# Re-layout reads of queries and keys: two of three row groups by one transfer

## The chip, the cores and the metric

The kernel runs on one core of one Trainium2 chip. The core has a matrix engine (TensorE, PE in the profile; its weight loads are PEld), a vector engine (DVE), a scalar engine (ACT), GpSimd (POOL) and SyncE (SP), which here only issues transfers; ACT issues some, too. All transfers run on 16 DMA engines. Each engine works through its own instructions in order and waits at semaphores for the others. The metric is device time in microseconds of one execution; the median of several runs is compared.

## The reference

One transformer layer on a prompt of 2048 tokens with 640 features, in float32:

```python
qkv = (layernorm(x) @ wqkv).reshape(B, S, 3, H, Dh)     # S=2048, H=32, Dh=20
scores = einsum("bhqd,bhkd->bhqk", q, k) * Dh ** -0.5
mask: 0 <= query - key < 256
h = x + (softmax(masked scores) @ v) @ wo
out = h + (gelu(layernorm(h) @ w_gate) * (layernorm(h) @ w_up)) @ w_down   # F=1536
```

Attention looks back over at most 256 keys, so a block of 128 queries needs its own block of keys and the two before it.

## The kernel before, in words

**Tiles.** Tokens are handled in 16 blocks of 128 (`B[j]`) and, for the projections of queries and keys, in 8 chunks of two blocks (`C[c]`, 256 columns, `CW`). Float32 operands are split in a high and a low float16 part, and a product is made of three: high by high, high by low, low by high.

**From projection to attention.** `qk(c, which)` computes the queries (`which` 0) or keys (1) of a chunk, 640 feature rows by 256 token columns, in three pieces. `qk_out` turns each into its two float16 parts and writes them, by transfers issued on ACT, to a DRAM tensor `d` of shape [640, 2, 256]: feature row, high or low, token. The weight columns are permuted so that the row is (a, d, i), with a the parity of the head (2), d the feature inside the head (20) and i the pair of heads (16).

`stack(c, which, d)`, the function of this change, reads `d` back in another layout. The tiles `qT` (one per chunk, two in turn) and `kT` (a ring of six blocks) have 128 rows. Rows 0 to 59 belong to the even heads, rows 64 to 123 to the odd ones: three groups of 20 rows, one row for each feature of a head. Along a row lie 16 heads of 256 tokens each. The groups of `qT` hold high, high, low and those of `kT` high, low, high, so one product over 60 rows gives all three terms. Rows 60 and 61 of `qT` later receive the rows' maxima in two parts (`max_transpose`, a small transfer on ACT), against a constant in `kT`. Each of the three groups of each half is one transfer: six for `qT`, six for `kT`, twelve per chunk. One transfer has 20 rows of 16 runs of 256 float16, 512 bytes each.

**Use.** `maxima` multiplies a block's queries with its window of keys to find the row maxima (DVE), `scores` makes the scores in transposed form for ACT's exponential, `value_lane` multiplies with the values, and `wo_block` projects and adds the residual. Afterwards the feed-forward runs over chunks of 512 tokens; it needs neither `qT` nor `kT`.

**What sets the order.** The whole order of instructions is made before the run. Lanes (generators) offer their next step with the engines that it needs and a function of when its data will be ready; the main loop at the end of `block_kernel` picks one step at a time. The class `Clock` keeps the planner's estimate of each engine's time: a transfer costs bytes / 150,000 us on a common line for 2-byte data on the chip, its issue 0.35 or 0.75 us, and no more than eight are thought of as in flight. In `stack` a first wait holds until the data is in DRAM and older blocks are scored (`B[2 * c - 3].scored`), so that the ring of `kT` has room; from chunk 2 on each transfer also waits until the line has at most `PACE` = 1 us of work left. When both stacks of a chunk are issued, its blocks go to the queue of `maxima`. All instructions pass through one helper, `call` in class `Engine`, so the profile gives line 199 for nearly all of them, and tiles tell them apart.

**On SP's queue**, in one order, stand these reads, the loads of x and of the weights, the turns of x to feature rows (transposing transfers), the loads of the residual and the writes of h. ACT issues the writes to `d` and the maxima.

Of the kernel before, what the change touches and what calls it, by code (L numbers as in the profile page):

```python
# [21 lines left out]
S, D, H, DH, F = 2048, 640, 32, 20, 1536  # L22
# [5 lines left out]
CW = 2 * P  # L28
# [225 lines left out]
def block_kernel(ctx: ExitStack, tc: tile.TileContext, x, wqkv, wo, wg, wu, wd, out):  # L254
    nc = Clock(tc.nc)
# [54 lines left out]
    def need(*reads, slots=(), when=None, eng="tensor"):  # L310

        def f():
            if when and not when() or any(opened[n] >= banks[n] for n in slots):
                return INF
            return max([nc.ready(reads, eng)]
                       + [nc.slot(psums[n], n, banks[n]) for n in slots])
        return f
# [432 lines left out]
    def qk_out(c, which, ts, ps, d, left):  # L750

        o = ps[:, :len(ts) * CW].rearrange("p (t n) -> p t n", n=CW)
        up = qs if c == which == 0 else _pow2(QE)
        yield on("scalar", ps, when=lambda: pos["qk"] < pos["qks"] + 2 and (c or pos["qs"]))
        pos["qk"] += 1
        st = nc.tile(wq, [P, 2, 2, CW], F16, "qks", 2)
        hi, lo = (st[:, :len(ts), i, :] for i in range(2))
        nc.scalar.activation(hi, o, AF.Copy, scale=up)
        yield on("vector", hi, after=ps)
        nc.vector.scalar_tensor_tensor(lo, o, up, hi, op0=ALU.mult, op1=ALU.subtract)  # L760
        done("mm")
        both = st[:, :len(ts)].rearrange("p t m n -> p t (m n)")
        yield on("scalar", both)
        nc.scalar.dma_start(d[ts[0] * P:(ts[-1] + 1) * P].rearrange("(t p) m n -> p t (m n)", p=P),
                            both)
        pos["qks"] += 1
        left[0] -= 1
        if not left[0]:
            side.append((LATE, stack(c, which, d)))

    def stack(c, which, d):
        yield ("sync",), need(d, when=lambda: pos["big"] == 2 and (W["q"].ready if c < 2 else
                                                                B[2 * c - 3].scored), eng="sync")
        if which == 0:
            C[c].qT = at("qT", [P, H // 2, CW], F16)
            for b in (2 * c, 2 * c + 1):
                B[b].mx = at("mxs", [P, H], F32, 4)
            to = C[c].qT
        else:
            s = 2 * c % RK  # L780
            to = kT[:, :, s:s + 2, :].rearrange("p i r n -> p i (r n)")
        for par in range(2):
            for m, i in enumerate(((0, 0, 1), (0, 1, 0))[which]):
                rows = slice(64 * par + DH * m, 64 * par + DH * m + DH)
                if c > 1:
                    yield ("sync",), lambda: nc.moved["sync"] - PACE
                nc.sync.dma_start(to[rows], d.rearrange("(a d i) m n -> a m d i n", a=2,
                                                        d=DH)[par, i])
        C[c].stacked += 1
        if C[c].stacked == 2:  # L790
            for b in (2 * c, 2 * c + 1):
                for pr in range(0, H // 2, pairs(b)):
                    heapq.heappush(maxq, (b, pr))
# [29 lines left out]
    def pairs(j):  # L823

        return 2 if j < 2 else 1
# [82 lines left out]
    def row_lane():  # L908
        while True:
            yield ("tensor",), row_need  # L910
            for f, n in list(row):
                f(n)
# [714 lines left out]
    rows = Lane(row_lane())  # L1627
# [89 lines left out]
```

## Time and profile before

| | |
|---|---|
| median of 3 runs | 1019.06 us (1015.35 to 1019.22) |
| the profiled execution | 1015.33 us, span 1013.6 us |
| mean granted TensorE clock | 0.997 |
| PE busy | 996.3 us, 98% of the span |
| DVE, ACT, POOL busy | 754.7, 442.5, 315.0 us |
| attention, by the use of qT and kT | to 566 us of the span |
| re-layout reads | 48 to qT, 48 to kT, 160 KB each |

How to read it: the page gives busy time per engine, then the chain of work that ended last, then the costliest groups. A row of a timeline is start, duration, engine (with a q: the engine's sequencer, as where it issues a transfer), line, operation, output<-inputs, shape and count; in brackets the idle time before it and what ended it. A row of a chain is start, duration and what. A row of a window table is the stretch and its length, busy time and instruction count of PE, PEld, DVE, ACT and POOL, then the granted clock, the DMA engines' mean share and GB/s. A row of the transfer view is queue, packets, MB and the packets' time as a share of 16 engines; the digits above it are tenths of that share in 40 slices.

### The profile page before, as it was taken

The page shows a single profiled execution, that of the slowest core. Times are in us where ns is not written, and L with a number is a line of the kernel's source. Part 1 is how long each engine was busy: PE and PEld are TensorE (multiplying, and loading weights), DVE is VectorE, ACT ScalarE, POOL GpSimd, SP SyncE. Part 2 cuts the span into 40 slices and gives each one's busy share as a digit, 9 for nine tenths or more (in the row PEclk, how much of TensorE's full clock was granted, in tenths as well). Part 3 has the DMA queues.
Part 4 walks back from the last instruction along what each step waited for, and adds up shares of the span by engine and source line. Part 5 has one row for each costly group of instructions (what it writes and reads, how often), then busy time and mean ns, then how long its engine had stood idle before and what let it go on. Part 6 is the DMA issues. An engine that isn't in the chain of part 4 may idle for free.

```text
span 1013.6 us, 30516 instructions
## 1 busy us (share of the span) xinstructions
PE 996.3 (98%) x12798; PEld 696.4 (69%) x12798; DVE 754.7 (74%) x2212; ACT 442.5 (44%) x711; POOL 315.0 (31%) x504
## 2 busy tenths in 40 slices
PE   8999999999999999999999999999999999999998
PEld 7876777666666776776655654577777777777776
DVE  7888999786667877676688687798888875544553
ACT  5516666654555555554567634432222212221220
POOL 7004344643344333332345311254313300000000
PEclk9999999999999999999999999999999999999999
DMA  8658775291271714236004342323453542222211
GB/s 308 148 127 177 185 163 167 67 166 41 71 133 39 143 55 88 64 79 188 18 29 133 68 130 92 98 107 116 144 187 102 148 142 78 79 103 80 78 53 52
DMA packets 105834, 112.67 MB, mean 111 GB/s; under 512 B 38368, under 2 KB 79584, under 8 KB 105696
## 3 DMA queue, kind: packets, MB, share of 16 engines
q1 hardware_dynamic: 93600, 99.97, 36.7%
q10 hardware_dynamic: 12096, 10.75, 3.5%
q8 instruction: 100, 1.64, 0.7%
q14 instruction: 38, 0.31, 0.1%
HBM read 73.73 MB, written 28.84 MB: 101 GB/s over the span
## 4 chain that ended last, share of the span: by engine, by line
PE 86%; DVE 7%; DMA 3%; ACT 2%; issue 1%; SPq 1%; POOL 0%; ACTq 0%; DVEq 0%
PE mm L199 44%; PE pv L199 12%; PE ra L199 12%; PE rb L199 10%; PE tp L199 7%; DVE junk L199 1%; DMA kT<-qk 1%; SPq L199 1%; DVE am L199 1%; DMA wst<-in_wu_dram 1%; DMA qT<-in_wqkv_dram 1%; DMA wst<-in_wg_dram 1%; ACT pt L199 1%; DVE ht L199 0%; DVE w1l L199 0%
## 5 line engine op out<-in xcount | busy, mean ns | idle before, releaser
L199 POOL TENSOR_SCALAR_AFFINE_SELECT pt<-pt 128x512 f32<-128x512 f32 x352 | 174.8, 512 | 297.0 <-ACT pt L199 281.3
L199 DVE CUSTOM_DVE_ANT_0 junk<-rb,band 128x320 bf16<-128x320 f32 x228 | 111.5, 489 | 53.4 <-PE rb L199 48.8
L199 ACT ACTIVATE pt<-ra,esc 128x640 f32<-128x640 f32 (+2 forms) x132 | 100.6, 770 | 74.3 <-PE ra L199 69.3
L199 DVE CUSTOM_DVE_ANT_0 junk<-ra,band 128x320 bf16<-128x320 f32 x220 | 107.7, 489 | 33.2 <-PE ra L199 26.8
L199 ACT ACTIVATE pt<-rb,esc 128x640 f32<-128x640 f32 (+2 forms) x124 | 94.1, 764 | 82.4 <-PE rb L199 73.2
L199 PE MATMUL pv<-pt,v 128*21 128x128 f32 x2880 | 104.7, 279 | 0.0
L199 PEld LDWEIGHTS <-ah 128*128 128x128 f16 x768 | 75.1, 98 | 29.2 <-issue 1.9
L199 ACT ACTIVATE gel<-gel,ffk 128x512 f32<-128x512 f32 x36 | 26.0, 722 | 134.3 <-DVE gel L199 134.3
L199 PEld LDWEIGHTS pv<-pt,v 128*21 128x21 f32 x2880 | 70.0, 101 | 9.9 <-issue 1.0
L199 PEld LDWEIGHTS <-ws 128*128 128x128 f16 x720 | 70.5, 98 | 8.1
L199 PEld LDWEIGHTS <-qT 60*64 60x64 f16 x1280 | 29.8, 104 | 61.0 <-issue 51.9
L199 PEld LDWEIGHTS <-kT 62*64 62x64 f16 x2880 | 63.4, 107 | 11.2 <-issue 7.5
L199 PEld LDWEIGHTS <-gu 128*128 128x128 f16 x440 | 41.9, 98 | 36.1 <-issue 2.5
L199 DVE SCALAR_TENSOR_TENSOR ht<-mm,ffk,ht 128x320 f32<-128x320 f32 x96 | 52.1, 545 | 13.7 <-PE mm L199 11.8
L199 ACT CAST ah<-gel 128x512 f16<-128x512 f32 x48 | 29.6, 617 | 68.7 <-DVE gel L199 68.6
L199 PE MATMUL mm<-xh,w1h 128*128 128x256 f16 x200 | 54.6, 273 | 0.8 <-DVE qks L199 0.8
L199 PE MATMUL mm<-xl,w1h 128*128 128x256 f16 x200 | 54.7, 274 | 0.0
L199 PE MATMUL mm<-xh,w1l 128*128 128x256 f16 x200 | 54.6, 273 | 0.0
L199 POOL TENSOR_TENSOR gelt<-gelt 128x256 f32<-128x256 f32 x18 | 15.3, 852 | 112.0 <-ACT gelt L199 111.9
L199 PE MATMUL mm<-w3h,oh 128*128 128x320 f16 x160 | 48.3, 302 | 1.4 <-DVE qks L199 1.4
L199 PE MATMUL mm<-w3l,oh 128*128 128x320 f16 x160 | 48.2, 301 | 0.0
L199 PE MATMUL mm<-w3h,ol 128*128 128x320 f16 x160 | 48.1, 300 | 0.0
(313 smaller groups left out, 2562.6 us busy)
## 6 DMA issues: line engine op xcount, KB each, us to landing
ws<-wsums SPq DMA_DIRECT2D x24, 640.0 KB
qk<-qks ACTq DMA_DIRECT2D x32, 256.0 KB
qT<-qk SPq DMA_DIRECT2D x48, 160.0 KB
kT<-qk SPq DMA_DIRECT2D x48, 160.0 KB
wsums<-ws SPq DMA_DIRECT2D x12, 640.0 KB
ht<-in_x_dram SPq DMA_DIRECT2D x16, 320.0 KB
h_dram<-ht SPq DMA_DIRECT2D x16, 320.0 KB
ht<-h_dram SPq DMA_DIRECT2D x16, 320.0 KB
```

Source lines behind the costliest of these rows:

```text
L199: r = real(*args, **kw)
```

## The change

For each half, the first two row groups are read by one transfer of 40 rows, the third by one of 20 as before. For `kT` the source is high and then low, read with the part as the outermost dimension; for `qT` it is the high part twice, a broadcast with an outermost dimension of step 0 and size 2. A chunk has 8 reads in place of 12: four of 320 KB, four of 160 KB. The bytes that land, and where, are the same.

```diff
+        parts_ = d.rearrange("(a d i) m n -> a m d i n", a=2, d=DH)
         for par in range(2):
-            for m, i in enumerate(((0, 0, 1), (0, 1, 0))[which]):
-                rows = slice(64 * par + DH * m, 64 * par + DH * m + DH)
+            for m, n in ((0, 2), (2, 1)):
+                rows = slice(64 * par + DH * m, 64 * par + DH * (m + n))
+                if n == 2:
+                    src = parts_[par] if which else parts_[par, 0].unsqueeze(0).to_broadcast(
+                        [2, DH, H // 2, CW])
+                else:
+                    src = parts_[par, 1 - which]
                 if c > 1:
                     yield ("sync",), lambda: nc.moved["sync"] - PACE
-                nc.sync.dma_start(to[rows], d.rearrange("(a d i) m n -> a m d i n", a=2,
-                                                        d=DH)[par, i])
+                nc.sync.dma_start(to[rows], src)
```

## The prediction, made before the change was run

> **What bounds the kernel now.** I read the page first, for the shares, the chain that ended last and the transfers.
>
> ```profile
> span 1013.6 us, 30516 instructions
> PE 996.3 (98%) x12798; PEld 696.4 (69%) x12798; DVE 754.7 (74%) x2212; ACT 442.5 (44%) x711; POOL 315.0 (31%) x504
> ...
> PE 86%; DVE 7%; DMA 3%; ACT 2%; issue 1%; SPq 1%; POOL 0%; ACTq 0%; DVEq 0%
> ...
> qk<-qks ACTq DMA_DIRECT2D x32, 256.0 KB
> qT<-qk SPq DMA_DIRECT2D x48, 160.0 KB
> kT<-qk SPq DMA_DIRECT2D x48, 160.0 KB
> ```
>
> TensorE works in 98% of the span, in an order that the planner wrote before the run. It has 1013.6 - 996.3 = 17.3 us of idle time, so a product that waits for late data is paid nearly in full: nothing behind it on TensorE can pass it. What matters is how much room each of the 96 re-layout reads (48 of qT, 48 of kT, 160 KB each) has before TensorE needs it. So I read SP's timeline for the issue of the reads, all eight qT stacks and the last reads of chunk 3's kT:
>
> ```profile
> 29.43 5.47 SPq L199 DMA_DIRECT2D qT<-qk  x6
> 61.82 6.16 SPq L199 DMA_DIRECT2D qT<-qk  x6
> 119.78 6.73 SPq L199 DMA_DIRECT2D qT<-qk  x6
> 200.49 3.17 SPq L199 DMA_DIRECT2D qT<-qk  x4
> 222.72 2.36 SPq L199 DMA_DIRECT2D kT<-qk  x3
> 272.21 4.72 SPq L199 DMA_DIRECT2D qT<-qk  x6
> 328.29 3.15 SPq L199 DMA_DIRECT2D qT<-qk  x4
> 393.02 4.73 SPq L199 DMA_DIRECT2D qT<-qk  x6
> 397.79 6.99 SPq L199 DMA_DIRECT2D kT<-qk  x6
> 449.08 4.71 SPq L199 DMA_DIRECT2D qT<-qk  x6
> ```
>
> Then TensorE's timeline for the first product that needs the whole of a chunk's qT and kT. The row-maximum products run block by block, 64 to a block and 128 in blocks 6, 7, 12 and 13, where the ring of key columns wraps; counted off in that order, the first of blocks 0, 2, ... 14 (in block 6 the first one on new columns) are:
>
> ```profile
> 51.81 0.31 PE L199 MATMUL ra<-kT,qT 60*64 60x128 f16 x8
> ...
> 88.80 0.33 PE L199 MATMUL ra<-kT,qT 60*64 60x320 f16 x4
> ...
> 159.46 0.38 PE L199 MATMUL ra<-kT,qT 60*64 60x320 f16 x4
> ...
> 229.55 0.32 PE L199 MATMUL rb<-kT,qT 60*64 60x64 f16 x3 [2.14 <-DMA kT<-qk]
> ...
> 297.31 0.33 PE L199 MATMUL ra<-kT,qT 60*64 60x320 f16 x3 [1.37 <-DMA kT<-qk]
> ...
> 355.82 0.33 PE L199 MATMUL ra<-kT,qT 60*64 60x320 f16 x4
> ...
> 413.05 0.33 PE L199 MATMUL ra<-kT,qT 60*64 60x256 f16 x8
> ...
> 476.56 0.33 PE L199 MATMUL rb<-kT,qT 60*64 60x320 f16 x4
> ```
>
> Two of the eight already wait for kT (2.14 and 1.37 us). The chain of waits gives the landing of the last read in these two, and one more thing:
>
> ```profile
> 224.34 5.08 DMA kT<-qk
> ...
> 286.98 3.72 DMA qk<-qks
> 292.29 4.99 DMA kT<-qk
> ```
>
> Chunk 3's last read lands at 224.34 + 5.08 = 229.42, chunk 4's at 297.28, each some 0.1 us ahead of the product. The reads are just in time. That is the profile's main message for this change: 12 reads a chunk have no room to become slower.
>
> **What the change removes and adds.** Per chunk, 12 reads become 8: four of 320 KB (the first two row groups) and four of 160 KB. Runs and bytes are the same, 512 bytes a run, 640 in a large read and 320 in a small one. The planner's price of the data is the same too, since the code takes bytes over 150,000 per us: 2.18 us for a large read against 2 x 1.09. So it will put the row maxima where they are now. It saves four issues on SP; 4.71 us for six is 0.79 each, at most 3.2 us a chunk. That is worth nothing to the landing, because the transfers are slower than the issues:
>
> ```profile
> q1 hardware_dynamic: 244, 0.12, 40.8%
> ```
>
> ```profile
> q1 hardware_dynamic: 1995, 0.99, 76.9%
> ```
>
> ```profile
> q10 hardware_dynamic: 29, 0.01, 11.0%
> ```
>
> ```profile
> q10 hardware_dynamic: 108, 0.10, 14.6%
> ```
>
> These are queue rows of the transfer view for four windows: 450.5 to 451.5 (a stack's first reads), 399 to 407 (reads of kT alone, densely queued), 161.48 to 161.78 (maxima written to qT's rows 60 and 61) and 453 to 456 (here the row of ACT's writes of q and k). The share is of 16 engines. First: 0.408 x 16 x 1.0 us / 244 = 27 ns a run where reads don't crowd. Second: 0.769 x 16 x 8 / 1995 = 49 ns a run, 12.3 records open at a time. I count ten engines, the even split of 20 rows that is nearest; 1995 / 8 / 10 = 25 runs per us and engine is 40 ns from run to run, and a read's 32 runs per engine take 1.28 us. Third: 0.110 x 16 x 0.3 / 29 = 18 ns a run of 256 bytes, and 0.110 x 16 = 1.8 open at a time. That transfer has two rows on the destination and 32 on the source, and it runs **two engines wide**.
>
> The new large read has 40 rows on the destination, but its source now walks two things outermost: hi and lo for kT, the same hi twice for qT (the broadcast with step 0). That two can't be folded into the 20 x 16 runs behind it. No row of before shows just this pair, 2 against 40. The nearest in shape is the third, 2 against 32, and I take it: two engines, 320 runs on each. The other end is ten engines and 64 runs each, which is today's load.
>
> The Trainium skill has a rule for this (DMA: Bandwidth & Descriptors, section "Why a DMA increments its semaphore by 16 and not by 1", and its "Rules for kernel authors", which warns of a leading broadcast): a transfer uses the largest number of engines up to 16 that divides both sides' slowest dimension. By it 20 rows get ten and 2 against 32 gets two, as the rows above have it, and 2 against 40 gets two. It speaks against this change. If it were not so for a broadcast or for a 40-row target, the sum below would be near zero.
>
> **The price of a large read.** 320 runs at 27 ns are 8.6 us (uncrowded), at 40 ns 12.8 us (ten engines crowding). Two engines crowd less than ten, so I take 8.6. I take the same pair of engines for all of them, as the successive reads of a stack queue now, so large reads follow each other. A small read behind it has 32 runs on the same engines, 0.9 to 1.3 us, say 1.2. A chunk's two stacks then need 4 x 8.6 + 4 x 1.2 = 39.2 us in place of 12 x 1.28 = 15.4. Around that stands a fixed part: chunk 3's last three reads were issued from 222.72 and landed by 229.42, 6.7 us, less 3 x 1.28 leaves 2.8. So kT is complete **42.0 us after the first qT issue**. The kT reads are issued before the qT stack's 19.6 us are over in nearly all chunks, so the engines don't idle between.
>
> **What TensorE waits**, chunk by chunk: issue + 42.0 - first product. Chunk 0: 71.4 - 51.8 = 19.6; 1: 103.8 - 88.8 = 15.0; 2: 161.8 - 159.5 = 2.3; 3: 242.5 - 229.6 = 12.9; 4: 314.2 - 297.3 = 16.9; 5: 370.3 - 355.8 = 14.5; 6: 435.0 - 413.1 = 21.9; 7: 491.1 - 476.6 = 14.5. The sum is 117.6 us. Each wait shifts everything behind it, the next issue too, since a stack waits for TensorE to be done with older blocks; so they add.
>
> Behind the waiting product, in TensorE's order, stand scores, values and dense products; ScalarE's exponentials and GpSimd's selects starve with them. On SP the queue is full sooner: six kT issues took 6.99 us at 397.79 against 4.73 for the six before, so SP waits when some seven reads of 32 runs are queued, and one large read brings 320 per engine. Turns of x, loads of x and h and writes of h behind the stack come late by up to the stack's time. Their readers stand behind the same TensorE wait, so I cost that at nothing; without this cover it would be the fourth case below. Two smaller terms. Other transfers share the two engines: a write of q or k is 256 runs, 16 per engine, and the fourth row gives 0.146 x 16 x 3 / 108 = 65 ns each, 1.0 us; about two such transfers per chunk fall in a stack, 8 x 2 = 16 us (0 to 40). And the clock, as the stages around the two waits of before show:
>
> ```profile
> 227.00:229.30 2.30, 0.41 (x6) 0.19 (x6) 0.00 (x0) 0.26 (x1) 0.28 (x1) 1.00 0.40 72
> 229.30:232.70 3.40, 3.15 (x50) 1.77 (x50) 1.00 (x4) 0.79 (x1) 0.00 (x0) 0.50 0.03 7
> ...
> 297.60:301.00 3.40, 3.40 (x78) 2.42 (x67) 1.00 (x4) 0.79 (x1) 1.42 (x3) 0.50 0.74 199
> ```
>
> After each, 3.4 us ran at a granted clock of 0.50, a loss of 1.7 us. Eight waits in place of two, some longer, at about 2 us each, less the 3.4 already there: 12 us (10 to 24). The Trainium skill (TensorE: Matmul & The Clock Gate, Part 1) says that the window is 3413 ns and free-running; by that a restart loses up to 3.4 us, the upper end.
>
> Sum: 117.6 + 16 + 12 = 146 us. The profiled execution took 1015.33 us (span 1013.6), 3.7 below the median of the runs, inside their spread. 1015 + 146 = **1161 us**.
>
> **The rivals.** (a) *The spread stays.* The large read goes over eight or ten engines by its 40 rows, so the engines' work per chunk is today's 15.4 us. Then SP's saved issues let the last kT read start earlier, and this decides where kT is awaited now: at most 2.14 + 1.37 us and the two half-clock losses, 3.4, come back; 1008 to 1016, say 1013, not slower. For it: 40 rows on the destination. Against: the row of 1.8 engines. (b) *Other pairs.* Large reads land on different engines and run side by side. Then kT comes 8.6 - 1.3 = 7.3 us later than now, less the room: about 0 to 7 us a chunk, 3 on average, 25 in all: 1040. No row tells which engines a transfer takes; the full queue at 397.79 speaks for a fixed set. (c) *Crowded price.* 40 ns a run: 4 x 320 x 13 ns = 16.6 us more per chunk, 8 x 16.6 = 133: 1294. For it: the dense row; against: only two engines push. (d) *Waits that add.* Transfers wait for unrelated ones to land: the write in the chain above, of a later chunk's q or k, landed at 286.98 + 3.72 = 290.70, and only then was chunk 4's kT issued:
>
> ```profile
> 290.71 2.31 SPq L199 DMA_DIRECT2D kT<-qk  x3
> ```
>
>  If ScalarE's writes so wait for large reads, exponentials stop before TensorE reaches the late kT, and part of a read's 8.6 us adds to the wait: 8 x 8 = 64, 1225.
>
> **How the numbers follow.** Forecast 0.63, with its own range of 1100 to 1225 (from the other-traffic and clock terms, and 25 to 30 ns a run); (a) 0.06, (b) 0.08, (c) 0.13, (d) 0.10. The likeliest gives 1161. From 1095 to 1290 I leave out (a), (b) and about half of (c). About 0.5% (5 us) is what a measurement here can tell from no change. Only (a) isn't slower: 0.02 faster, 0.04 within; slower 0.94.
>
> **What would show it.** Right: in attention the transfer digits fall to 1 or 2 for stretches of ten us and more; issues of 320 KB x16 each for qT and kT; eight waits of TensorE for qT or kT of some 15 to 22 us, 120 to 150 us in total; TensorE busy about as long as now, hence near 86% of the span; the chain's DMA share above 10%; PEclk 0.50 around each wait; nothing lost after 566. The two engines are wrong if the digits stay at 6 and 7 in the stacks and no TensorE wait exceeds 3 us; the price is wrong if a stack's landing is nearer 28 us than 20; the sum is wrong if TensorE stops earlier, for ScalarE.

## The result

| | before | after |
|---|---|---|
| median, us (6 runs each, lowest to highest) | 1015.38 (1013.71 to 1019.22) | 1188.34 (1186.06 to 1189.43) |
| profiled execution, span, us | 1013.6 | 1187.3 |
| PE busy, us | 996.3 | 1019.8 |
| PE idle (span less busy), us | 17.3 | 167.5 |
| mean granted TensorE clock | 0.997 | 0.931 |

The ratio is 1.169, with a 95% interval of 1.166 to 1.172: the changed kernel is 17% slower. The forecast was 1161 us, with its own range of 1100 to 1225. Of the runs below, one of experiment 5 (1055.83 us, at a granted clock of 0.939) fell in a slower state that some executions show, and is not counted.

The page of the changed kernel, in the lines that answer to those shown of before (the third is PE's busy tenths over 40 slices of the span):

```profile
span 1187.3 us, 30473 instructions
PE 1019.8 (86%) x12798; PEld 708.2 (60%) x12798; DVE 749.4 (63%) x2212; ACT 443.4 (37%) x711; POOL 313.4 (26%) x504
...
PE   8757696796696696792994999999999999999998
...
PE 67%; SPq 15%; DMA 9%; DVE 5%; ACT 2%; issue 2%; ACTq 0%; DVEq 0%
...
qT<-qk SPq DMA_DIRECT2D x16, 320.0 KB
kT<-qk SPq DMA_DIRECT2D x16, 320.0 KB
```

TensorE runs as many products as before (x12798). Of the 173.7 us by which the span grew, 167.5 - 17.3 = 150.2 are time in which it does nothing, and 1019.8 - 996.3 = 23.5 are products that take longer. The slices after the 22nd, which ends at 653 us, stand at 9, and the last at 8.

Nearly all the idle time lies in eight places. Windows of 50 us, each from the first read of a chunk's queries on (stretch and length, busy time and count of PE, PEld, DVE, ACT, POOL, then the granted clock, the transfers' share, GB/s):

```profile
29.00:79.00 50.00, 27.58 (x216) 21.23 (x215) 20.37 (x68) 13.81 (x29) 1.65 (x3) 0.76 0.37 75
86.00:136.00 50.00, 31.43 (x378) 20.98 (x376) 24.94 (x111) 10.35 (x24) 4.35 (x7) 0.81 0.44 94
167.00:217.00 50.00, 33.87 (x473) 23.08 (x466) 30.20 (x110) 17.21 (x29) 10.96 (x18) 0.92 0.44 108
267.00:317.00 50.00, 31.56 (x524) 22.05 (x514) 25.94 (x92) 16.56 (x27) 12.20 (x23) 0.80 0.45 87
351.00:401.00 50.00, 28.03 (x548) 19.04 (x547) 20.77 (x78) 14.90 (x23) 10.50 (x22) 0.78 0.34 81
437.00:487.00 50.00, 30.02 (x487) 20.61 (x488) 20.65 (x74) 15.71 (x25) 10.57 (x22) 0.81 0.38 74
523.00:573.00 50.00, 28.87 (x531) 19.13 (x529) 18.29 (x70) 15.65 (x24) 11.11 (x24) 0.80 0.18 51
603.00:653.00 50.00, 33.07 (x573) 22.64 (x561) 18.05 (x67) 14.54 (x24) 9.38 (x21) 0.83 0.32 94
```

Eight windows, one for each chunk, hold 400 - 244.4 = 155.6 of the 167.5 us. TensorE is idle for 22.4, 18.6, 16.1, 18.4, 22.0, 20.0, 21.1 and 16.9 us in them.

Chunk 6 shows how it goes. First SP's timeline (the two groups of issues), then TensorE's (the three products that end a stop):

```profile
523.69 16.82 SPq L199 DMA_DIRECT2D qT<-qk  x4
...
540.55 18.74 SPq L199 DMA_DIRECT2D kT<-qk  x4
```

```profile
545.54 0.27 PE L199 MATMUL ra<-kT,qT 60*64 60x256 f16 x3 [3.10 <-DMA qT<-qk]
...
554.86 0.26 PE L199 MATMUL ra<-kT,qT 60*64 60x64 f16 x1 [9.05 <-DMA kT<-qk]
...
564.10 0.32 PE L199 MATMUL ra<-kT,qT 60*64 60x64 f16 x3 [8.98 <-DMA kT<-qk]
```

The chain of waits of the changed kernel has, for that last stop:

```profile
550.81 13.25 DMA kT<-qk
```

The kT is complete at 550.81 + 13.25 = 564.06, which is 40.4 us after the first issue at 523.69. Before, the six reads of this chunk's queries took SP 4.73 us to issue; now the four take 16.82. SP itself is held up at its issues.

The transfer view between 536 and 544, with 40 slices of 0.2 us:

```profile
DMA  1111111111111111111411111133477521111111
GB/s 41 41 41 41 44 41 41 41 44 41 41 41 41 41 44 41 41 41 44 123 41 41 41 41 44 41 92 95 131 202 195 136 31 15 20 20 36 41 41 41
```

A digit of 1 is 10 to 20% of 16 engines; two engines are 12.5%. 41 GB/s over two engines is 20.5 GB/s each, or 512 / 20.5 = 25 ns a run of 512 bytes. The trace does not name the engines, so that they are two is worked out from these rates; in the window 536 to 539.5, 283 runs and a share of 14.3% make 0.143 x 16 = 2.3 open at a time, where the dense reads of before had 12.3. The 92 to 202 GB/s in between is the small read of 160 KB: the six slices from 92 on hold about 0.2 us x 851 GB/s = 170 KB.

### The profile page after: what moved, and what is told of

Same layout as the page of the kernel before. It is cut to its first block, busy times and chain, and to the rows that moved or that the text cites. A ratio compares the mean times of both kernels' runs of the same rounds, so it can differ in the third digit from the quotient of the medians.

```text
span 1187.3 us, 30473 instructions
## 1 busy us (share of the span) xinstructions
PE 1019.8 (86%) x12798; PEld 708.2 (60%) x12798; DVE 749.4 (63%) x2212; ACT 443.4 (37%) x711; POOL 313.4 (26%) x504
## 4 chain that ended last, share of the span: by engine, by line
PE 67%; SPq 15%; DMA 9%; DVE 5%; ACT 2%; issue 2%; ACTq 0%; DVEq 0%
PE mm L199 34%; SPq L199 15%; PE ra L199 10%; PE pv L199 10%; PE rb L199 8%; PE tp L199 6%; DMA kT<-qk 5%; DMA qT<-qk 1%; DVE junk L199 1%; DMA xl<-xp 1%; DMA qT<-mT 1%; DMA qT<-in_wqkv_dram 0%; ACT pt L199 0%; DMA wst<-in_wu_dram 0%; DVE am L199 0%
## 5 line engine op out<-in xcount | busy, mean ns | idle before, releaser
L199 DVE CUSTOM_DVE_ANT_0 junk<-ra,band 128x320 bf16<-128x320 f32 x210 | 102.8, 490 | 147.3 <-PE ra L199 142.3
L199 ACT ACTIVATE pt<-rb,esc 128x640 f32<-128x640 f32 (+2 forms) x119 | 90.1, 763 | 162.9 <-PE rb L199 152.9
L199 DVE CUSTOM_DVE_ANT_0 junk<-rb,band 128x320 bf16<-128x320 f32 x238 | 116.4, 489 | 42.9 <-PE rb L199 37.2
L199 PE MATMUL ra<-kT,qT 60*64 60x320 f16 (+4 forms) x604 | 42.0, 292 | 112.1 <-DMA kT<-qk 109.0
L199 ACT ACTIVATE pt<-ra,esc 128x640 f32<-128x640 f32 (+2 forms) x137 | 104.6, 770 | 88.5 <-PE ra L199 77.4
L199 PE MATMUL pv<-pt,v 128*21 128x128 f32 x2880 | 107.6, 284 | 0.0
L199 PEld LDWEIGHTS <-kT 62*64 62x64 f16 x2880 | 66.5, 110 | 38.5 <-issue 33.2
L199 PE MATMUL ra<-qT,kT 62*64 62x128 f16 (+1 forms) x1548 | 42.1, 212 | 18.5 <-ACT pt L199 16.5
L199 PE MATMUL rb<-kT,qT 60*64 60x320 f16 (+4 forms) x676 | 43.0, 287 | 7.9 <-ACT pt L199 7.9
```

What stands on the lines that cost most here:

```text
L199: r = real(*args, **kw)
```

## The experiments

The kernel before was run beside each of them: 1015.41 us (with the first four), 1015.66 (with those of one chunk, the price and the layout) and 1016.62 (the last three). Ratios are against that.

**1. As large and as few, but wide.** From the changed kernel: a large read walks 40 feature rows in one sequence.

```diff
                 if n == 2:
-                    src = parts_[par] if which else parts_[par, 0].unsqueeze(0).to_broadcast(
-                        [2, DH, H // 2, CW])
+                    src = d.rearrange("(x i) m n -> m x i n", x=2 * DH)[0]
```

> Eight reads a chunk as after the change, the large ones of 40 rows, 640 runs and 320 KB at the same places, but from a source with nothing walked twice outermost: 40 consecutive groups of 16 rows of the high part. The rows so hold other values (the low part and one half's heads are left out of the first two groups), the amount of work is the same. Theory (the large read is confined to two engines because its source walks two things outermost): the read goes over ten engines, the transfer digits are 5 to 8 in the stacks, TensorE waits for kT at most a few us in all, 1010 to 1022 us. Rival (fewer, larger reads come later as such, or the plan has changed): still 1170 to 1200 us.

Measured: 1017.99 us (1016.04 to 1021.29, 10 runs), ratio 1.0026 (1.0007 to 1.0045), as the theory had it. Its transfer view from 449 to 457 (the same 0.2 us slices), and its group of row-maximum products, with the idle time before them and what ended most of it:

```profile
DMA  7632346655666777667777999988777987776654
```

```profile
L199 PE MATMUL ra<-kT,qT 60*64 60x320 f16 (+4 forms) x652 | 40.6, 281 | 0.8 <-DVE mxs L199 0.8
```

The same 8 reads of the same sizes, with mostly 6 to 9 in the digits in place of 1, cost next to nothing: the 652 row-maximum products of that group wait 0.8 us in all, for DVE. So neither the number nor the size of the reads makes the 173 us; the digits show that it goes with how many engines a read is spread over. It shows too what the change would have been worth had the width stayed: four fewer issues a chunk give no gain (the planner's order differs a little, with 12889 products for 12798, so the 2.6 us need not be a price of the reads).

**2. As many and as small, but narrow.** From the kernel before: twelve reads of 160 KB, each walking ten feature rows twice, so that the source's outermost size is two.

```diff
-                nc.sync.dma_start(to[rows], d.rearrange("(a d i) m n -> a m d i n", a=2,
-                                                        d=DH)[par, i])
+                half = d.rearrange("(a d i) m n -> a m d i n", a=2, d=DH)[par, i][:DH // 2]
+                nc.sync.dma_start(to[rows], half.unsqueeze(0).to_broadcast(
+                    [2, DH // 2, H // 2, CW]))
```

> Twelve reads of 20 rows and 320 runs as before the change, but each from a source that walks the first ten rows of its group twice (outermost 2, step 0), so half of each group's values are replaced by the other half's. Theory (width): 160 runs on each of two engines, 160 x 27 ns = 4.3 us a read, 12 x 4.3 = 52 us a chunk in place of 39 after the change; kT is complete some 55 us after the first issue, 10 to 13 us later than after, 8 x 11.5 = 92 us more: about 1275 us (1240 to 1310). Rival (merging is the cost, not the width): as before, about 1015 us.

Measured: 1252.04 us (2 runs), ratio 1.231 (1.227 to 1.235), in the expected range. From its SP timeline and its waits (total, times, longest):

```profile
29.39 21.41 SPq L199 DMA_DIRECT2D qT<-qk  x6
```

```profile
PE ra L199 <- DMA kT<-qk: 103.2, 9, 19.8
```

All reads narrow is worse than two thirds of the bytes narrow, and one stack is 21.41 us of issuing where the kernel before has 5.47. The width alone, with nothing merged, makes the loss.

**3 and 4. Keys alone, queries alone.** From the changed kernel: only one of the two stacks has large reads.

```diff
-            for m, n in ((0, 2), (2, 1)):
+            for m, n in ((0, 2), (2, 1)) if which else ((0, 1), (1, 1), (2, 1)):
...
-                    src = parts_[par, 1 - which]
+                    src = parts_[par, ((0, 0, 1), (0, 1, 0))[which][m]]
```

With `if not which` it is the queries.

> Only kT by a large read (source high, then low; no broadcast), qT by three. Theory (two engines for both kinds): a stack of kT takes 19.6 us, kT is complete 30.1 us after the first issue of qT or 22.4 us after its own, whichever is later; against the products of before this gives 10.7, 9.2, 0, 2, 5, 6.5, 10 and 8.3 us, 52 in all, with clock and other traffic 70: about 1085 us (1060 to 1110). Rival (only the broadcast of step 0 is slow): about 1015 us.

> Only qT by a large read (the broadcast), kT by three. Theory (two engines for both kinds): kT queues behind qT's 19.6 us, complete 30.1 us after the first issue; 7.7, 3.1, 0, 1, 5, 2.6, 10 and 2.6 us, 32 in all, with clock and other traffic 45: about 1060 us (1035 to 1090). Rival (the broadcast is the whole loss): about 1188 us, as after.

Measured: keys 1098.58 us, ratio 1.080 (1.076 to 1.084); queries 1096.42, ratio 1.078 (1.075 to 1.082); 2 runs each. So the broadcast with step 0 and the real pair of high and low cost the same, and 83.2 + 81.0 = 164 of the 173 us add up. The keys came as expected; the queries were expected 36 us lower, and 1096 is above the expected range, which ended at 1090. The kernel with the queries alone has these waits of TensorE (total, times, longest), and then one of ACT's:

```profile
PE ra L199 <- DMA kT<-qk: 32.0, 8, 7.8
PE ra L199 <- ACT pt L199: 11.2, 2, 9.4
PE rb L199 <- DVE mxs L199: 10.8, 2, 10.4
PE rb L199 <- ACT pt L199: 8.2, 2, 7.8
```

```profile
ACT xp L199 <- DMA xl<-xp: 34.3, 4, 14.1
```

kT's lateness is 32 us, just what the sum counted, but TensorE stops for another 11.2 + 10.8 + 8.2 = 30.2 us on ACT and DVE, where before it had 1.2 for DVE's `mxs` and nothing for ACT's `pt`. ACT is late because it waits for turns of x, and DVE once stood 11.59 us (up to 104.17) for a load of `wo`; both stand behind the reads on SP's queue. The sum had those at nothing.

**5 and 6. One chunk alone.** From the changed kernel, with `if c == 2` and `if c == 6` in the same place, and the other chunks read as before. By the prediction's sum chunk 2 has the most room, 2.3 us of wait, and chunk 6 the least, 21.9.

> Large reads in chunk 2 alone, twelve small ones in the other seven. The prediction's sum gave this chunk 2.3 us of waiting, since its kT had 14 us of room, and cost the transfers held up on SP's queue at nothing: by it 1017 to 1021 us. After the change TensorE stood still for 16 us in this chunk. Theory now (a turn of x held up behind the large reads keeps the buffer xp, and ScalarE stops at its next cast into it, ahead of exponentials that TensorE needs): 1028 to 1038 us, with a ScalarE wait of over 10 us for the turn xl<-xp. Rival (those 16 us came only from chunks 0 and 1 having shifted things): 1015 to 1021 us.

> Large reads in chunk 6 alone. The sum gave it 21.9 us, after the change TensorE stood still for 21.1 us there. Theory (the chunks' waits are independent and add; the plan has no room here): 1015 + 21 + 2 to 4 of half clock = 1036 to 1042 us. Rival (a single late chunk is caught up by the next seven): under 1025 us.

Measured: chunk 2 1035.22 us (3 runs), ratio 1.019 (1.016 to 1.023); chunk 6 1036.35 (2 runs), ratio 1.020 (1.016 to 1.025). Chunk 6 stops in the same three places as in the changed kernel (TensorE's timeline):

```profile
413.03 0.27 PE L199 MATMUL ra<-kT,qT 60*64 60x256 f16 x3 [1.41 <-DMA qT<-qk]
...
422.32 0.26 PE L199 MATMUL ra<-kT,qT 60*64 60x64 f16 x1 [9.01 <-DMA kT<-qk]
...
431.62 0.32 PE L199 MATMUL ra<-kT,qT 60*64 60x64 f16 x3 [9.04 <-DMA kT<-qk]
```

1.41 + 9.01 + 9.04 = 19.5 us, where it had 21.1 among eight: in this chunk the wait doesn't depend on the others, and it isn't caught up behind it; the time is in the expected range. Chunk 2 costs as much, and by another way. Its time is in the expected range, too, but the wait for the turn of x, expected at over 10 us, is only one of three. The timelines of SP, DVE, ACT (with its queue's issue) and TensorE with large reads in chunk 2 alone:

```profile
139.19 9.07 SPq L199 DMA_DIRECT2D h_dram<-ht  x1
```

```profile
153.33 0.61 DVE L199 TENSOR_SCALAR ht<-ht,lmvh,lyh 128x640 f32<-128x640 f32 x1 [8.38 <-DMA h_dram<-ht]
```

```profile
153.38 0.37 ACTq L199 DMA_DIRECT2D qk<-qks  x1
153.84 0.39 ACT L199 ACTIVATE qks<-mm 128x256 f16<-128x256 f32 x1 [9.25 <-DMA h_dram<-ht]
...
165.81 0.72 ACT L199 CAST xp<-xt 128x640 f16<-128x640 f32 x1 [7.12 <-DMA xl<-xp]
```

```profile
154.00 1.11 PE L199 MATMUL tp<-ident,ht 128*128 128x128 f32 x4 [7.68 <-DVE sw L199]
...
168.81 0.48 PE L199 MATMUL ra<-qT,kT 62*64 62x128 f16 x12 [6.45 <-ACT pt L199]
```

A write of h stands behind the large reads on SP's queue; SP takes 9.07 us to issue it. DVE normalises `ht` in place and can't start until it has left, waits 8.38 us and then does the normalization for which TensorE stands 7.68 us. ACT stands 9.25 us, until it issues a write of q or k at 153.38, and the trace puts that down to the same landing. Then a turn of x comes late, ACT waits 7.12 us for the buffer of `xp`, and TensorE stops for its exponentials. No stop here is for qT or kT. These are not "behind the same TensorE wait": in chunk 2 there is no such wait.

**7. The planner told the price.** From the changed kernel: a large read costs 8.6 us in the plan's arithmetic, in place of 2.18.

```diff
+            if out.space != DRAM and out.partition_size() == 2 * DH:
+                return 8.6
             wide = mybir.dt.size(out.dtype) == 4 or out.space == DRAM
```

> The reads of the change, but the planner is told 8.6 us for a large one in place of 2.2, so that it can put other work ahead of the products on the late kT. Theory (the loss is a plan that counts on kT just in time, and 39 us of reads fit into a chunk's 60 us of other work): chunks 2 to 7 lose most of their waits, chunks 0 and 1 keep theirs (some 40 us), 1050 to 1120 us. Rival (the ring of key columns lets no stack start earlier and there is nothing to fill with): over 1160 us.

Measured: 1129.51 us (2 runs), ratio 1.112 (1.107 to 1.117), 9.5 above the expected range. Busy times from the page (the span is 1125.7 us), and the products on the identity that the planner puts where it sees TensorE idle (x221 before):

```profile
PE 1060.9 (94%) x13409; PEld 739.4 (66%) x13409; DVE 756.3 (67%) x2212; ACT 441.2 (39%) x711; POOL 311.4 (28%) x504
```

```profile
L199 PE MATMUL pv<-ident x832: 219/219/311, 2.5 to 110.1; 128*128 128x128 f16 x167
```

The idle time falls from 167.5 to 1125.7 - 1060.9 = 64.8 us, and busy time grows by 41.1, with 832 - 221 = 611 more filling products in the first 110 us. 59 of the 173 us come back. A third of the loss was thus an order made for another price; the rest isn't won by this order.

**8 and 10. A layout in which both can be had.** The DRAM tensor becomes [half, part, feature row, token], so that two row groups are 40 rows in one sequence (the last two groups of qT, the first two of kT). Each projected piece then needs more writes: 96 in place of 48.

```diff
-        d = dram.tile([D, 2, CW], F16, name=f"qk{c}{which}")
+        d = dram.tile([2, 2, D // 2, CW], F16, name=f"qk{c}{which}")
...
-            for m, n in ((0, 2), (2, 1)):
+            for m, n in (((0, 1), (1, 2)), ((0, 2), (2, 1)))[which]:
...
+                src = parts_[par][:n * DH]
```

The tenth kernel has this layout and these writes with twelve reads of one row group.

> Eight reads a chunk with the reference's values: the DRAM tensor is laid out as half, part, feature row, token, so high and low of one half follow each other without a gap, and both large reads take them as 40 rows in one sequence (kT's first two groups, qT's last two). qT's rows then are runs of 8 KB. The writes have runs of 512 bytes and are 96 in place of 48. Theory (width decides): over ten engines, no large waits, 1008 to 1022 us; faster than before by a few us if the two waits for kT of before go. Rival (the merge itself costs): over 1100 us. The doubled writes cost ScalarE some 18 us of issue; if they are on the path, 1020 to 1035 us.

> The twelve reads of before with the DRAM layout of the wide reads, so only the doubled writes (96 of 512-byte runs in place of 48 of 1 KB) and qT's runs of 8 KB are left of that kernel. Theory (its 52 us over before come from the doubled writes: more issues on ACT, and a plan that puts the first stacks later and fills with idle products): 1055 to 1080 us. Rival (they come from the wide large reads after all): 1010 to 1025 us.

Measured: 1067.93 us (1066.24 to 1069.50, 6 runs), ratio 1.051 (1.048 to 1.054) with eight reads; 1070.97 (2 runs), ratio 1.053 (1.049 to 1.057) with twelve. The expectation for the eighth fell; that for the tenth held. SP's timeline of the eighth (chunk 3's queries, at 200.49 before):

```profile
252.97 1.43 SPq L199 DMA_DIRECT2D qT<-qk  x4
```

By chunk 3's reads the kernel is 252.97 - 200.49 = 52.5 us behind, which is the whole loss. It comes with the writes and what the planner makes of them, not with the reads, since it is there with twelve reads too. Both kernels have 741 filling products in the first 97 us, where before had 221. Which of the writes' issues, their small size and the plan sets it was not taken apart. Between the two, eight wide reads for twelve make no difference that these runs can tell.

**9. One of chunk 2's causes removed.** From the kernel with large reads in chunk 2 alone: the write of h is issued by ACT, in all chunks, so that it doesn't stand behind the reads.

```diff
-        yield ("sync",), need(b.h, eng="sync")
-        nc.sync.dma_start(h_dram[j * P:(j + 1) * P, :], b.h)
+        yield ("scalar",), need(b.h, eng="scalar")
+        nc.scalar.dma_start(h_dram[j * P:(j + 1) * P, :], b.h)
```

> Large reads in chunk 2 alone, and the write of h to DRAM issued on ACT in place of SP. With SP the write stood behind a large kT read, DVE waited 8.4 us for it (it normalises h in place), and TensorE stood still for 7.7 us and then 6.5 us for a turn of x. Theory (transfers held up behind large reads on SP's queue, with no cover in this chunk): the 7.7 us go, the 6.5 us for the turn stay, 1024 to 1031 us. Rival (the write is late because the two engines are busy, whatever queue it comes from, or the later kT takes its place): 1033 to 1040 us.

Measured: 1034.11 us (4 runs), ratio 1.017 (1.014 to 1.020): the rival's number. DVE's wait for h is gone, and ACT's timeline has

```profile
155.11 0.38 ACT L199 ACTIVATE qks<-mm 128x256 f16<-128x256 f32 x1 [7.63 <-DMA kT<-qk]
```

At the issue of its write of q or k (at 154.63), ACT stands until a read of kT lands, a transfer that has nothing to do with that write; and it still waits 5.80 us for the turn of x later. With this one wait removed, others take its place, so it alone does not set chunk 2's cost. A second buffer for `xp`, which might remove the turn's wait, was not tried.

**11. Four engines.** As the second, with the first five feature rows walked four times.

```diff
-                half = d.rearrange("(a d i) m n -> a m d i n", a=2, d=DH)[par, i][:DH // 2]
+                half = d.rearrange("(a d i) m n -> a m d i n", a=2, d=DH)[par, i][:DH // 4]
                 nc.sync.dma_start(to[rows], half.unsqueeze(0).to_broadcast(
-                    [2, DH // 2, H // 2, CW]))
+                    [4, DH // 4, H // 2, CW]))
```

> Twelve reads of 20 rows and 320 runs, each from a source that walks the first five rows of its group four times, so three quarters of each group's values are replaced. Theory (the width is what divides both sides' outermost sizes, here four; 80 runs per engine at 27 ns are 2.2 us): 26 us of reads a chunk against 15 before and 52 at width two; kT complete 29 us after the first issue, 25 us of waits, with clock and held-up transfers 1035 to 1065 us. Rival (any broadcast source is as slow as width two): about 1250 us.

Measured: 1069.64 us (2 runs), ratio 1.052 (1.047 to 1.056), 5 above the expected range and far below the rival's 1250. SP's timeline and the transfer view from 500 to 515 (slices of 0.375 us):

```profile
29.37 10.86 SPq L199 DMA_DIRECT2D qT<-qk  x6
```

```profile
GB/s 74 67 79 86 85 87 87 86 82 79 85 203 344 227 117 89 86 89 87 86 104 63 71 76 82 82 67 314 321 135 82 82 76 93 322 109 87 89 87 78
```

The slices at 82 to 89 GB/s are twice the 41 of two engines. The first six reads take SP 5.47, 10.86 and 21.41 us as the outermost size of the source goes from twenty to four to two, and the kernel takes 1015, 1070 and 1252 us. The rule of the Trainium skill that the prediction named (DMA: Bandwidth & Descriptors, section "Why a DMA increments its semaphore by 16 and not by 1") gives ten, four and two engines for these; the rates of the last two agree with it, and the trace has no separate row for ten.

## Why the prediction was right, and where it was wrong

**Two engines, 320 runs each.** Right. The row chosen as nearest, 2 against 32, was the right one; the rate in the stacks is that of two engines at 25 ns a run, where the prediction took 27. The experiments 1, 2 and 11 move the width alone and the time goes with it. Rival (a), the width staying, has its own measurement in experiment 1: 1018 us, where 1013 was given. Its gain from fewer issues isn't there.

**The same pair of engines.** The digits stay at 1 through the stacks, so large reads didn't run side by side on other engines; rival (b) falls. Rival (c), the crowded price, falls with the 25 ns.

**kT complete 42.0 us after the first issue.** 40.4 in chunk 6; the chain of waits has these landings for chunks 1 and 3:

```profile
119.54 14.65 DMA kT<-qk
...
308.96 4.99 DMA kT<-qk
```

with the first issues of their chunks, on SP's timeline, at

```profile
86.44 17.75 SPq L199 DMA_DIRECT2D qT<-qk  x4
...
267.14 7.46 SPq L199 DMA_DIRECT2D qT<-qk  x3
```

That makes 47.8 and 46.8 us. To the start of the product that ends the last stop it is 45.2, 45.5, 45.3 and 44.0 us in chunks 0, 4, 5 and 7. Six chunks are 2 to 6 us above 42.0, and chunk 6 is 1.6 below; chunk 2 has no stop for kT to read it from. The term for other traffic on the two engines allowed 2 a chunk, and the mean over the seven is 3.0: about the right size, though no run shows that other traffic is the cause.

**What TensorE waits.** The prediction added 117.6 + 16 = 133.6 us of idle time; it was 150.2. Most of the difference is one chunk: chunk 2 was given 2.3 us and stood for 16.1. The step that failed is "their readers stand behind the same TensorE wait, so I cost that at nothing". In chunk 2 of the changed kernel, as in experiment 5, DVE stands for a write of h:

```profile
201.16 0.61 DVE L199 TENSOR_SCALAR ht<-ht,lmvh,lyh 128x640 f32<-128x640 f32 x1 [8.66 <-DMA h_dram<-ht]
```

The room of qT and kT was computed rightly, and what stood behind them on the queue had less. It is not chunk 2 alone that stops early. TensorE's waits in the changed kernel (total, times, longest):

```profile
PE ra L199 <- DMA kT<-qk: 109.0, 12, 12.8
PE ra L199 <- ACT pt L199: 16.5, 3, 9.2
PE rb L199 <- DVE mxs L199: 8.7, 1, 8.7
PE rb L199 <- ACT pt L199: 8.3, 2, 7.9
PE tp L199 <- DVE sw L199: 8.0, 1, 8.0
```

41.5 us end on ACT or DVE: 8.73 in chunk 1 (DVE there waits for a load of `wo`), 7.97 and 6.12 in chunk 2, 9.24 in chunk 3 and 7.91 in chunk 5 (ACT waits for turns of x), the rest in short waits. Stops ahead of the late kT are what rival (d) forecast, and they came in four chunks, mostly through turns and loads and not ScalarE's writes; its price, 8 us on top in each of the eight, isn't there; and the sign that "the sum is wrong if TensorE stops earlier, for ScalarE" came true. In chunks 1, 3 and 5 it didn't come on top: they stand 3.6, 5.5 and 5.5 us over the sum, and kT landed 5.8, 4.8 and 3.3 us later than the sum had it. There the early stop took the place of a part of the wait for kT, so the number came out near although only 112 us of waiting end on kT or qT. Where kT had room, in chunk 2, what is behind it is paid by itself; and in experiment 4, where kT's wait is short, the stops for ACT and DVE are most of the 36 us by which the expectation was too low.

**Half clock.** Predicted 12 us (10 to 24), measured 23.5, the upper end. The prediction counted one restart a chunk; TensorE's timeline has two or three stops of over 1 us in each. Half of it lies in chunks 0 to 2, as two windows with about the same number of products show, before (29 to 200) and after (29 to 267):

```profile
29.00:200.00 171.00, 168.46 (x2432) 122.14 (x2431) 147.23 (x549) 98.18 (x175) 57.11 (x87) 1.00 0.64 151
```

```profile
29.00:267.00 238.00, 180.25 (x2440) 127.20 (x2438) 144.57 (x550) 98.27 (x175) 56.92 (x87) 0.87 0.43 108
```

180.25 - 168.46 = 11.8 us for 8 products more, at a granted clock of 0.87 for 1.00. With chunk 6 alone (experiment 6) the sum of PE's busy time did not grow, 996.4 for 996.3. That isn't a restart without a price: the 3.4 us from 432.60, behind its last stop, ran at a granted clock of 0.53, but the two stretches that ran at 0.50 before, from 229.30 and from 297.60, had 1.00 and 0.75 there.

**The signs.** Transfer digits of 1, 320 KB x16 twice, PE at 86%, and nothing lost behind attention were as stated. Eight waits for qT or kT of 15 to 22 us, 120 to 150 us in total, were not: there are 13 of at most 12.8 us, 112.1 in total, and none in chunk 2. The chain's DMA share was 9%, not above 10%; SPq has 15% of the chain, where before had 1%. The prediction saw that SP would wait with its queue full, but not that this would be what the chain shows.

## What to carry to other kernels

Before merging transfers, look at the outermost size on both sides of the new one, source and broadcast too: here a two in that place left a read two engines, by its rate, where it had some ten, and no saving in issues could pay for it. Take the time from issue to need of each transfer from the trace first; where it is nothing, a slower transfer is paid nearly in full, here once in nearly every chunk. And ask of everything behind a slow transfer on its queue, writes and turns included, who waits for it: the room of the transfer itself isn't the least room on that queue.

## What the runs showed that I had not expected

**The issue itself takes the time.** The issue of six 160 KB reads takes SP 5.47 us at twenty rows, 10.86 at four and 21.41 at two outermost, and a single write of h behind large reads took 9.07 us. With a slow transfer ahead, the issuing engine's instruction is where the time shows, and a reader of the DMA share alone would miss it.

**A write that waits for a stranger.** ACT's write of q or k stood 7.63 us for a read of kT on another queue (experiment 9), and 9.25 us for a write of h (experiment 5). The data don't connect them. What the trace shows is the wait; that the transfers share a semaphore on which their landings are counted is my reading of it, and no run here took it apart.

**Fewer transfers were worth nothing.** 64 reads in place of 96, with the width kept, gained nothing in two layouts: experiment 1 is 2.6 us slower than before, and 8 and 10 can't be told apart.
